# Blockwise attention before a mixture of experts: q and k loaded as runs of six tokens into 128 partitions, two heads' queries interleaved

## The chip, the cores and the metric

One core of one Trainium2 chip runs the whole program in one launch. The time is device microseconds of that launch, from the first to the last instruction of the core and what lies around it. Lower is better. Every figure is the median of several runs, or comes from one execution that the hardware profiler recorded.

## The reference

Three things are computed, one after the other: attention in chunks with some context and memory, a mixture of eight experts of which each token takes one, and a dense feed-forward layer.

```python
B, H, S, D = 4, 8, 768, 64            # chunk 32, context 16 to the left and 8 to the right, 8 memory keys
for c in range(S // 32):
    k_full = concatenate([mem_k, k[:, :, 32*c-16 : 32*c+40]])
    v_full = concatenate([mem_v, v[:, :, 32*c-16 : 32*c+40]])
    scores = matmul(q[:, :, 32*c : 32*c+32], k_full.T) / sqrt(D)
    a = exp(scores - max(scores)); a = a / (sum(a) + 1e-9)
    out[:, :, 32*c : 32*c+32] = matmul(a, v_full)
x = out.transpose(0, 2, 1, 3).reshape(B * S, H * D)        # 3072 x 512
e = argmax(x @ w_gate + modality_bias[modality_id])
x = gate_w * (maximum(x @ w1[e], 0) @ w2[e])               # 8 experts, 512 -> 1024 -> 512
out = elu(x @ w_in) @ w_out                                # 512 -> 2048 -> 512
```

All tensors are float32.

## The kernel before

`program` (from line 1140) holds an `Attention`, a `Routing`, a `Moe` and a `Moe2` object. The order of all instructions is written out by hand: inside `tc.manual_schedule` each engine runs its instructions in the order in which the Python code issues them, and semaphores keep the dependences. DMAs issued with `nc.sync` stand in SP's queue in that same order.

**Items and units.** Attention works on 8 items, an item being one batch and four heads (`self.items`), and on 24 units, a unit being one third of an item's 24 chunks, 8 chunks (`self.units`). "Item 3" is the fourth. `Attention.run` (line 426) goes through the units. In each it issues scores (`sc`), the transposition and the product with v of earlier units (`tr`, `pv`), the softmax (`sm`, `exp`), and some steps of the next item's q and k, taken from the list `pend` by the table `pops`: all eight steps of item ix + 1 run during item ix.

**Loads.** `load_qk(ix, j)` (line 82) loads k (j = 0) or q (j = 1) of an item: 768 tokens of four heads. Each partition takes a run of RUN = 8 tokens of each head, so 768 / 8 = 96 partitions are filled, and a piece of memory that lies in one stretch is 8 tokens x 64 x 4 bytes = 2,048 bytes. The arena tile `ld`, 128 x 6,144 floats, holds three such buffers, used in turn. `start` loads k and q of item 0, v of item 0 and k of item 1. In `run`, at the first unit of item ix, the v of item ix + 1 and the k of item ix + 2 are loaded (k first where ix is 0). The q of item ix + 1 is loaded by `tsteps(ix)`, behind the four k steps, since its buffer is the one that k of item ix leaves. `load_v` (line 93) brings v in pieces of 256 bytes, in 10 DMAs an item, of which the two long ones write 32 partitions each; `copy_v` on POOL then copies the overlapping part of the windows.

**Steps.** `transposed` (line 218) turns a loaded head with TensorE, two tokens (128 floats) at a time: RUN / 2 = 4 transposes of 96 partitions into one bank of PSUM. `k_step` copies half of the bank to kT on ACT and half on DVE. `q_step` copies both halves to qT on ACT. `k_next` makes the second half of each chunk's key window (POOL, and ACT for the memory keys).

**The block diagonal of queries.** Two heads x = 0, 1 share a matmul: the upper 64 partitions of qT hold head 0, the lower ones head 1, and the columns of the other head are zero (`zeros`, line 124, once per buffer). qT is `[128, 2, NC, 2, CH]`: for each chunk 32 columns of head 0, then 32 of head 1. `sc` (line 253) uses these 64 columns as the weights of one matmul, so scores come out with the 32 queries of head 0 above the 32 of head 1. After the softmax `tr` transposes them into `pt`, and `pv` (line 296) takes each head's 32 adjacent columns of `pt` as the weights of its product with v.

**After attention.** The buffers of `ld` become three buffers of 2,048 floats for expert weights (`wr.give("raw", ...)`, line 766), in the order 1, 2, 0. `Moe.load_w` fills them from SP's queue, the first behind the last load of attention.

Of the kernel before, what the change touches and what calls it, by code (L numbers as in the profile page):

```python
# [7 lines left out]
FP32 = dt.float32  # L8
# [12 lines left out]
CH, NC, NM, WIN = 32, 24, 8, 64  # L21
LEFT, RIGHT = 16, 8
TOK = LEFT + CH + RIGHT
RUN = 8
E = 8
ROW = 513
SLOT, SMALL = 384, 256
# [9 lines left out]
class Banks:  # L37


    def __init__(self, *T):  # L40
        self.T, self.n = T, 0
# [11 lines left out]
class Attention:  # L53
# [28 lines left out]
    def load_qk(self, ix, j):  # L82

        b, Q = self.items[ix]
        t = self.arena["ld"].rearrange("p (s h x) -> p s h x", s=3, h=4)[0:self.S // RUN, (2 * ix + j) % 3]
        self.nc.sync.dma_start(out=t, in_=(self.k, self.q)[j][b, 4 * Q:4 * Q + 4].rearrange("h (p r) d -> p h (r d)", r=RUN))
        self.loads[ix, j] = t

# [43 lines left out]
    def start(self):  # L132
        nc, const, S, D, B, NT = self.nc, self.const, self.S, self.D, self.B, self.NT
        t = lambda shape, name, d=FP32: const.tile(shape, d, name=name)
        self.vw, self.qT, self.kT = [None] * 3, [None] * 2, [None] * 2
        for s in range(3):
            self.vw[s] = (const, self.last)[s].tile([128, 2, NC, 130], FP32, name=f"vw{s}") if s < 2 else self.arena["vw"].rearrange("p (a c e) -> p a c e", a=2, e=130)
        for s in range(2):
            p = (const, self.last)[s]
            self.qT[s] = p.tile([128, 2, NC, 2, CH], FP32, name=f"qT{s}")  # L140
            self.kT[s] = p.tile([128, 2, 2, LEFT + S + RIGHT], FP32, name=f"kT{s}")
        self.x = self.rk.tile([128, 6, 512], FP32, name="x")
        mk = self.x[:, 4, 0:128].rearrange("p (x d) -> p x d", d=64)
        self.memT = t([128, 4 * B, NM], "memT")
        zero = t([128, 1], "zero")
        for j in range(2):
            self.load_qk(0, j)
        for x in range(2):
            nc.scalar.dma_start(out=mk[:, x], in_=bass.AP(
                tensor=self.mem_k.tensor, offset=self.mem_k.offset + x * NM * D, ap=[[2 * NM * D, 4 * B], [D, NM], [1, D]]))  # L150
        ident = self.ident = self.K["ident"]
        identity(nc, const, ident)
        for s in range(3):
            self.v_edges(s)
        self.load_v(0)
        self.load_qk(1, 0)
        nc.vector.memset(zero, 0.0)
        self.zeros(0)
        self.v_blocks(0, 1, nc.gpsimd)
        nc.scalar.copy(out=self.vw[0][self.half[1], :, :, 0:65], in_=zero[self.half[1]].unsqueeze(2).unsqueeze(3).to_broadcast([64, 2, NC, 65]))  # L160
        nc.vector.memset(self.vw[0][self.half[0], :, :, 64:65], 1.0)
        self.zeros(1)
        self.wgp = self.rk.tile([128, 4, 32], FP32, name="wgp")
        nc.gpsimd.memset(self.wgp, 0.0)
        for hh in range(2):
            self.v_blocks(1, hh, nc.gpsimd)
        pm = self.ps_t.tile([128, 128], FP32, name="ps_qk")
        nc.tensor.transpose(pm, mk.rearrange("p x d -> p (x d)"), ident)
        nc.vector.tensor_copy(out=self.memT.rearrange("p n m -> p (n m)"), in_=pm)
        for st in self.tsteps(0):  # L170
            st()
        self.copy_v(0)
        nc.gpsimd.dma_start(out=self.wgp[:, :, 0:8], in_=self.wg.rearrange("(c p) e -> p c e", p=128))
        self.mi = self.x[0:NT, 5, 0:256].bitcast(I32).rearrange("t (p two) -> t p two", two=2)
        nc.gpsimd.dma_start(out=self.mi, in_=self.mid.bitcast(I32).rearrange("(t p two) -> t p two", p=128, two=2))
        self.mb = const.tile([128, 2, E], FP32, name="mb")
        nc.gpsimd.dma_start(out=self.mb.rearrange("p m e -> p (m e)"), in_=self.mbias.rearrange("m e -> (m e)").unsqueeze(0).to_broadcast([128, 2 * E]))
# [54 lines left out]

    def q_step(self, ix, x, y):
        ps = self.transposed(ix, 1, x, y)
        o = self.qT[ix % 2][self.half[x], y, :, x].rearrange("p c (i s r) -> p c i s r", r=2, s=RUN // 2)
        for r in range(2):
            self.nc.scalar.copy(out=o[:, :, :, :, r], in_=ps[self.half[r]].rearrange("p s (c i) -> p c i s", i=CH // RUN))

    def k_next(self, ix):

# [7 lines left out]
    def tsteps(self, ix):  # L248
        xy = [(x, y) for y in range(2) for x in range(2)]
        steps = [lambda a=a: self.k_step(ix, *a) for a in xy]  # L250
        return steps + [lambda: (self.k_next(ix), ix + 1 < len(self.items) and self.load_qk(ix + 1, 1), self.q_step(ix, *xy[0]))] + [lambda a=a: self.q_step(ix, *a) for a in xy[1:]]


    def sc(self, u, gg):
        ix, G = self.units[u]
        s = ix % 2
        if gg == 0:
            self.scs[u] = self.ps_s.tile([128, 4, 2, WIN], FP32, name="ps_sc")
        ps = self.scs[u]
        for y in range(2):  # L260
            for i in range(4):
                c = 8 * G + 4 * gg + i
                j = 64 * (i % 2)
                self.nc.tensor.matmul(out=ps[j:j + 64, 2 * gg + i // 2, y], lhsT=self.qT[s][:, y, c].rearrange("p x q -> p (x q)"), rhs=self.kT[s][:, y, :, CH * c:CH * c + CH],
                                      start=True, stop=True, tile_position=(0, j))

    def sm(self, u):
# [28 lines left out]
    def pv(self, u):  # L296
        nc = self.nc
        ix, G = self.units[u]
        b, Q = self.items[ix]
        pt = self.ptt.pop(u)  # L300
        po = self.ps_v
        for gg in range(2):
            for hp in range(2):
                for j in range(4):
                    nc.tensor.matmul(out=po[32 * j:32 * j + 32, gg, 130 * hp:130 * hp + 130], lhsT=pt[:, 2 * gg + j // 2, 64 * (j % 2) + 32 * hp:64 * (j % 2) + 32 * hp + 32],
                                     rhs=self.vw[ix % 3][:, hp, 8 * G + 4 * gg + j, :], start=True, stop=True, tile_position=(0, 32 * j))
        x = self.x[:, 2 * G:2 * G + 2]
        pw = po[:, :, 0:260].rearrange("p g (h e) -> p g h e", e=65)
        den = self.wk.tile([128, 2, 4], FP32, name="den")
        nc.vector.tensor_scalar(out=den, in0=pw[:, :, :, 64], scalar1=1e-9, scalar2=None, op0=ALU.add)  # L310
        nc.vector.reciprocal(out=den, in_=den)
        for gg in range(2):
            nc.vector.tensor_tensor(out=x[:, gg, 256 * Q:256 * Q + 256].rearrange("p (b a d) -> p a b d", d=64, a=2), in0=pw[:, gg, :, 0:64].rearrange("p (a b) d -> p a b d", a=2),
                                    in1=den[:, gg].rearrange("p (a b) -> p a b", a=2).unsqueeze(3).to_broadcast([128, 2, 2, 64]), op=ALU.mult)
# [111 lines left out]
    def run(self, more):  # L426
# [30 lines left out]
        for u in range(N):  # L457
            ix, G = self.units[u]
# [3 lines left out]
                for _ in range(min(pops[i], len(pend))):  # L462
                    pend.pop(0)()
            if G == 0:
                loads = [(self.load_v, ix + 1), (self.load_qk, ix + 2, 0)]
                for f, i, *a in loads[::-1] if ix == 0 else loads:
                    if i < NI:
                        f(i, *a)
            if G == 0 and ix + 1 < NI:
# [283 lines left out]
class Moe:  # L753


    def __init__(self, ctx, tc, banks, turn, arena, xs, rt, w1, w2, x2T, idd, ident):
        self.nc, self.tc, self.ctx = tc.nc, tc, ctx
        self.__dict__.update(xs=xs, rt=rt, w1=w1, w2=w2, x2T=x2T, idd=idd, ident=ident)
        self.wr, self.gp, self.wp, self.xp, self.hp, self.op = self.rings = [Ring(b) for b in (3, 2, 4, 2, 3, 1)]
        self.ps_x, self.ps_h = self.turns = turn, Banks(*banks[3:5])  # L760
        self.acc = [t[:, 0:SLOT] for t in (banks[2], banks[5], banks[6][:, 0], banks[6][:, 1])]
        self.W, self.X, self.R, self.G, self.Hd, self.raw = {}, {}, {}, {}, {}, {}
        self.N = {}


        self.wr.give("raw", *[arena["ld"][:, 2048 * i:2048 * i + 2048] for i in (1, 2, 0)])
        self.gp.give("G", *[arena["vw"][:, 3 * ROW * i:3 * ROW * i + 3 * ROW].rearrange("p (a c) -> p a c", c=ROW) for i in range(2)])
        self.op.give("x2o", arena["vw"][:, 6 * ROW:6 * ROW + KC * SLOT].rearrange("p (d n) -> p d n", n=SLOT))
        for n in ("xh", "xl", "whi1", "wlo1"):
            (self.xp if n[0] == "x" else self.wp).give(n, arena[n])  # L770
# [522 lines left out]
```

## Time and profile before

| | us |
|---|---|
| median of 3 runs | 1042.43 |
| fastest and slowest of them | 1040.51, 1044.9 |
| the profiled execution, whole | 1038.87 |
| its span, first to last instruction | 1037.1 |
| PE busy in the span | 982.1 (95%) |
| DVE, ACT, POOL busy | 571.0, 431.3, 212.7 |
| attention's first to last load of k or q issued (line 86) | 0.8 to 121.2 |
| attention's first to last scores matmul (line 264) | 17.0 to 165.5 |

The page of a profile cuts the span into 40 slices of some 26 us and gives each engine's busy share in tenths. Attention takes about the first seven. A timeline lists instructions of one engine in order of time; the bracket behind a row tells how long the engine stood idle before it and which instruction or transfer ended that. The granted clock is the share of TensorE's full speed that the chip gave. TensorE's weight load (PEld) and matmul (PE) are separate records, and a float32 matmul that is no transpose appears as two of each.

### The profile page before, as it was taken

To read this page: it belongs to the slowest core of one execution; us is meant where nothing else is said; L and a number is where in the kernel's file an instruction comes from. 1 tells how busy PE (TensorE), PEld (TensorE's weight loads), DVE (VectorE), ACT (ScalarE), POOL (GpSimd) and SP (SyncE) were. 2 spreads that over 40 slices of the span, in tenths; PEclk is the share of its full clock that TensorE was granted. 3 is DMA by queue.
4 is the path that set the end of the run, shared out by engine and by line. 5 is a ranking of instruction groups with operands and counts; after the bars stand their busy time and mean duration, and the time that the engine had idled before them with its cause. 6 is when DMAs were issued, how large, how long until landed. Compare 5 with 4: busy or idle time off the path is not lost.

```text
span 1037.1 us, 16438 instructions
## 1 busy us (share of the span) xinstructions
PE 982.1 (95%) x6350; PEld 845.1 (81%) x6350; DVE 571.0 (55%) x1056; ACT 431.3 (42%) x797; POOL 212.7 (21%) x202
## 2 busy tenths in 40 slices
PE   5778979989999999999999999999999999999998
PEld 4656667879999999999778888888888888888886
DVE  5536677857998999755555333333333433343332
ACT  5656656355666566555444222222222222222221
POOL 7565451532432432310000000010010001001001
PEclk9889989999999999999999999999999999999999
DMA  9999982388978987775433100010110001001001
GB/s 176 138 203 162 215 216 70 85 273 295 340 274 289 354 303 272 237 228 182 147 101 112 41 31 21 21 41 1 41 41 1 0 1 41 1 1 41 1 1 41
DMA packets 95969, 130.59 MB, mean 126 GB/s; under 512 B 36586, under 2 KB 65340, under 8 KB 93832
## 3 DMA queue, kind: packets, MB, share of 16 engines
q1 hardware_dynamic: 85176, 97.56, 35.0%
q0 software_dynamic: 8816, 29.71, 8.5%
q10 hardware_dynamic: 1888, 2.16, 0.6%
q8 instruction: 53, 0.87, 0.4%
q14 instruction: 36, 0.29, 0.1%
HBM read 101.59 MB, written 27.81 MB: 125 GB/s over the span
## 4 chain that ended last, share of the span: by engine, by line
issue 32%; PE 17%; POOL 2%; POOLq 0%; ACT 0%; DVE 0%; ACTq 0%
PE b L1060 9%; PE b L1078 8%; POOL out_dram L1087 2%; POOLq L1287 0%; DVE g L1066 0%; ACT g L1064 0%; ACT o L1084 0%; DVE g L1065 0%; POOLq L1087 0%; PE b L1096 0%; ACT gh L1069 0%; ACTq L1084 0%; ACTq L1064 0%
## 5 line engine op out<-in xcount | busy, mean ns | idle before, releaser
L1065 DVE TENSOR_SCALAR g<-g 128x512 f32<-128x512 f32 x96 | 41.0, 427 | 247.7 <-ACT g L1064 247.5
L1064 ACT ACTIVATE g<-b 128x512 f32<-128x512 f32 x96 | 57.3, 597 | 260.8 <-PE b L1060 260.8
L1078 PE MATMUL b<-woh,gl 128*128 128x512 f32 x384 | 152.0, 396 | 0.0
L1078 PE MATMUL b<-woh,gh 128*128 128x512 f32 x384 | 152.0, 396 | 0.0
L1078 PE MATMUL b<-wol,gh 128*128 128x512 f32 x384 | 151.8, 395 | 0.0
L1087 POOL DMA_INDIRECT out_dram<-o,idc x24 | 23.4, 976 | 549.3 <-ACT o L1084 337.0
L1069 ACT CAST gh<-g 128x512 fp32r<-128x512 f32 x96 | 59.6, 621 | 118.0 <-DVE g L1066 118.0
L1060 PE MATMUL b<-c_xh,wih 128*128 128x512 f32 x384 | 104.4, 393 | 2.0 <-PEq L1243 2.0
L1060 PE MATMUL b<-c_xh,wil 128*128 128x512 f32 x384 | 103.9, 392 | 0.0
L1060 PE MATMUL b<-c_xl,wih 128*128 128x512 f32 x384 | 103.9, 392 | 0.0
L1070 DVE TENSOR_TENSOR gl<-g,gh 128x512 fp32r<-128x512 f32 x96 | 66.5, 693 | 65.9 <-ACT gh L1069 37.1
L858 PE MATMUL b<-hh,whi 128*128 128x384 f32 (+1 forms) x288 | 95.0, 330 | 0.8 <-ACT xT L331 0.8
L858 PE MATMUL b<-hl,whi 128*128 128x384 f32 (+1 forms) x288 | 94.7, 329 | 0.0
L858 PE MATMUL b<-hh,wlo 128*128 128x384 f32 (+1 forms) x288 | 94.6, 328 | 0.0
L807 DVE TENSOR_TENSOR wlo<-arena_ld,whi 128x512 fp32r<-128x512 f32 x128 | 85.4, 707 | 11.5 <-ACT whi L806 11.0
L1060 PEld LDWEIGHTS b<-c_xh,wih 128*128 128x128 f32 x384 | 72.0, 188 | 19.0 <-issue 2.2
L1078 PEld LDWEIGHTS b<-wol,gh 128*128 128x128 f32 x384 | 72.2, 188 | 17.5
L1078 PEld LDWEIGHTS b<-woh,gl 128*128 128x128 f32 x384 | 72.2, 188 | 17.4
L1078 PEld LDWEIGHTS b<-woh,gh 128*128 128x128 f32 x384 | 72.1, 188 | 17.1
L1060 PEld LDWEIGHTS b<-c_xl,wih 128*128 128x128 f32 x384 | 72.1, 188 | 16.3
L1060 PEld LDWEIGHTS b<-c_xh,wil 128*128 128x128 f32 x384 | 72.1, 188 | 16.3
L847 ACT ACTIVATE hh<-b 128x384 fp32r<-128x384 f32 (+1 forms) x72 | 34.5, 479 | 93.6 <-PE b L843 92.3
(248 smaller groups left out, 1687.9 us busy)
## 6 DMA issues: line engine op xcount, KB each, us to landing
arena_ld<-in_moe_w_dram SPq DMA_DIRECT2D x74, 512.0 KB
d<-in_moe_w_in_dram SPq DMA_DIRECT2D x8, 1024.0 KB
d<-in_moe_w_out_dram SPq DMA_DIRECT2D x8, 1024.0 KB
arena_ld<-in_k_dram SPq DMA_DIRECT2D x8, 768.0 KB
arena_ld<-in_q_dram SPq DMA_DIRECT2D x8, 768.0 KB
xs<-x POOLq DMA_DIRECT2D x12, 512.0 KB, 7.4
x2T<-arena_vw SPq DMA_DIRECT2D x32, 192.0 KB
vw<-in_v_dram SPq DMA_DIRECT2D x12, 376.0 KB
```

The lines of the kernel that those rows point to most:

```text
L807: self.nc.vector.tensor_tensor(out=lo[:, c], in0=r, in1=hi[:, c].bitcast(FP32), op=ALU.subtract)
L847: nc.scalar.activation(out=hh, in_=ps, func=ACTF.Relu)
L858: self.nc.tensor.matmul(out=self.acc[d][:, 0:self.N.get(s, SLOT)], lhsT=a[:, c:c + 128], rhs=b, start=f == 0 and i == 0, stop=f == NF - 1 ...
L1060: nc.tensor.matmul(out=ps, lhsT=a[:, kc, 128 * r:128 * r + 128], rhs=x[:, kc], start=n == 0, stop=n == 11)
L1064: nc.scalar.activation(out=g, in_=ps, func=ACTF.Exp)
L1065: nc.vector.tensor_scalar(out=g, in0=g, scalar1=1.0, scalar2=-1.0, op0=ALU.min, op1=ALU.add)
L1069: nc.scalar.copy(out=gh, in_=g)
L1070: nc.vector.tensor_tensor(out=gl, in0=g, in1=gh.bitcast(FP32), op=ALU.subtract)
L1078: self.nc.tensor.matmul(out=self.acc[t], lhsT=a[:, c], rhs=w[:, r], start=f == 0 and i == 0, stop=f == self.NF2 - 1 and i == 2)
L1087: ins = nc.gpsimd.indirect_dma_start(out=self.out, out_offset=bass.IndirectOffsetOnAxis(ap=self.idc[:, 4 * b + t:4 * b + t + 1], axis=0), ...
```

## The change

RUN becomes 6: 768 / 6 = 128 partitions are filled and a piece is 6 x 64 x 4 = 1,536 bytes. The tile `ld` is cut into four buffers of 1,536 floats instead of three of 2,048: one for k and one for q of even items, and the same of odd items. So q no longer waits for the buffer of the k one item before it, and `load_qk` leaves `tsteps`: `run` loads k and q of item ix + 2 together, behind v of item ix + 1, or ahead of it where ix is 0. A step has 3 transposes of 128 partitions. qT becomes `[128, 2, S, 2]`: for each token the column of head 0, then that of head 1. So the copies into it write every fourth float (every second before), the zeros every second float, and the weights of `pv` are every second column of `pt`. The buffers for expert weights are handed over in the order 0, 1, 2.

```diff
-RUN = 8
+RUN = 6
...
     def load_qk(self, ix, j):
         b, Q = self.items[ix]
-        t = self.arena["ld"].rearrange("p (s h x) -> p s h x", s=3, h=4)[0:self.S // RUN, (2 * ix + j) % 3]
+        t = self.arena["ld"].rearrange("p (s j h x) -> p s j h x", s=2, j=2, h=4)[:, ix % 2, j]
...
-            self.qT[s] = p.tile([128, 2, NC, 2, CH], FP32, name=f"qT{s}")
+            self.qT[s] = p.tile([128, 2, S, 2], FP32, name=f"qT{s}")
...
         self.load_v(0)
-        self.load_qk(1, 0)
+        for j in range(2):
+            self.load_qk(1, j)
...
     def q_step(self, ix, x, y):
         ps = self.transposed(ix, 1, x, y)
-        o = self.qT[ix % 2][self.half[x], y, :, x].rearrange("p c (i s r) -> p c i s r", r=2, s=RUN // 2)
+        o = self.qT[ix % 2][self.half[x], y, :, x].rearrange("p (i s r) -> p i s r", r=2, s=RUN // 2)
         for r in range(2):
-            self.nc.scalar.copy(out=o[:, :, :, :, r], in_=ps[self.half[r]].rearrange("p s (c i) -> p c i s", i=CH // RUN))
+            self.nc.scalar.copy(out=o[:, :, :, r], in_=ps[self.half[r]].rearrange("p s i -> p i s"))
...
-        return steps + [lambda: (self.k_next(ix), ix + 1 < len(self.items) and self.load_qk(ix + 1, 1), self.q_step(ix, *xy[0]))] + [lambda a=a: self.q_step(ix, *a) for a in xy[1:]]
+        return steps + [lambda: (self.k_next(ix), self.q_step(ix, *xy[0]))] + [lambda a=a: self.q_step(ix, *a) for a in xy[1:]]
...
-                ... lhsT=self.qT[s][:, y, c].rearrange("p x q -> p (x q)"), ...
+                ... lhsT=self.qT[s][:, y, CH * c:CH * c + CH].rearrange("p q x -> p (q x)"), ...
...
-                    ... lhsT=pt[:, 2 * gg + j // 2, 64 * (j % 2) + 32 * hp:64 * (j % 2) + 32 * hp + 32], ...
+                    ... lhsT=pt[:, 2 * gg + j // 2, 64 * (j % 2) + hp:64 * (j % 2) + 64:2], ...
...
             if G == 0:
-                loads = [(self.load_v, ix + 1), (self.load_qk, ix + 2, 0)]
-                for f, i, *a in loads[::-1] if ix == 0 else loads:
+                qk = [(self.load_qk, ix + 2, j) for j in range(2)]
+                v = [(self.load_v, ix + 1)]
+                for f, i, *a in v + qk if ix else qk + v:
...
-        self.wr.give("raw", *[arena["ld"][:, 2048 * i:2048 * i + 2048] for i in (1, 2, 0)])
+        self.wr.give("raw", *[arena["ld"][:, 2048 * i:2048 * i + 2048] for i in range(3)])
```

SP's queue around the v of item 1, which is `vw1`. The rows are those of k1, q1, k2, then v of item 1 and q2; in brackets stands the semaphore that the DMA waits for, PE's where its buffer must first have been transposed:

```order
-L86 DMA arena_ld_89<-in_k_dram 96x4x512 [waits DMAHW6_49]
-L86 DMA arena_ld_89<-in_q_dram 96x4x512 [waits DMAHW7_49,PE_49]
-L86 DMA arena_ld_89<-in_k_dram 96x4x512 [waits DMAHW0_49,PE_49]
-L101 DMA vw1_111<-in_v_dram 32x47x64 [waits DMAHW1_49]
...
+L86 DMA arena_ld_89<-in_k_dram 128x4x384 [waits DMAHW6_49]
+L86 DMA arena_ld_89<-in_q_dram 128x4x384 [waits DMAHW7_49]
+L86 DMA arena_ld_89<-in_k_dram 128x4x384 [waits DMAHW0_49,PE_49]
+L86 DMA arena_ld_89<-in_q_dram 128x4x384 [waits DMAHW1_49,PE_49]
+L101 DMA vw1_111<-in_v_dram 32x47x64 [waits DMAHW2_49]
...
-L86 DMA arena_ld_89<-in_q_dram 96x4x512 [waits DMAHW3_49,PE_49]
```

q2 moved from behind all of v of item 1 to ahead of it, and q1 lost its wait for PE. From item 3 on the order of the loads is the same as before.

PE's queue in unit 2, while the steps of item 1 are made; `b0` to `b2` are the banks of PSUM that the steps use. Before:

```order
L291 MATMUL b5_84<-ident_68,p_268 128x128 x4
L223 MATMUL b0_79<-ident_68,arena_ld_89 128x96 x4
L223 MATMUL b1_80<-ident_68,arena_ld_89 128x96 x4
L264 MATMUL b3_82<-kT0_113,qT0_112 64x64 x8
L223 MATMUL b2_81<-ident_68,arena_ld_89 128x96 x4
```

And with the change, where lines stand one lower:

```order
L292 MATMUL b5_84<-ident_68,p_261 128x128 x4
L224 MATMUL b0_79<-ident_68,arena_ld_89 128x128 x3
L224 MATMUL b1_80<-ident_68,arena_ld_89 128x128 x3
L265 MATMUL b3_82<-kT0_113,qT0_112 64x64 x8
L224 MATMUL b2_81<-ident_68,arena_ld_89 128x128 x3
```

No step moved on PE; each has three transposes of 128 columns where it had four of 96.

## Rows read from the trace of the kernel before

**Rows 1.** The page, busy tenths in 40 slices of the span.

```profile
PE   5778979989999999999999999999999999999998
...
DMA  9999982388978987775433100010110001001001
```

**Rows 2.** Waits of PE, 0 to 182 us: us in total, times, longest.

```profile
PE b L223 <- DMA arena_ld<-in_q_dram: 2.9, 1, 2.9
```

**Rows 3.** Timeline of SP's queue: start us, us, instruction.

```profile
16.84 0.31 SPq L86 DMA_DIRECT2D arena_ld<-in_k_dram  x1
17.64 0.31 SPq L101 DMA_DIRECT2D vw<-in_v_dram  x1
...
37.26 0.32 SPq L86 DMA_DIRECT2D arena_ld<-in_q_dram  x1
...
47.58 0.41 SPq L86 DMA_DIRECT2D arena_ld<-in_k_dram  x1
```

**Rows 4.** Line 86 by itself: duration ns min/median/max, first and last start us.

```profile
L86 SPq DMA_DIRECT2D arena_ld<-in_k_dram x8: 312/318/467, 0.8 to 119.0; - x8
```

**Rows 5.** Transfers, 19 to 28 us, in 40 slices.

```profile
GB/s 118 182 273 264 273 219 228 191 237 273 237 255 191 228 218 237 255 200 237 273 246 209 200 237 273 237 246 219 219 237 282 228 182 233 292 226 246 133 129 131
```

**Rows 6.** Transfers, 168 to 174 us, in 40 slices, and what was issued.

```profile
GB/s 0 0 0 0 0 0 0 0 61 205 198 232 280 375 396 369 369 382 355 259 109 137 164 150 164 273 396 396 423 314 369 328 232 109 0 0 0 0 0 0
...
arena_ld<-in_moe_w_dram SPq DMA_DIRECT2D x2, 512.0 KB
```

**Rows 7.** Timeline of PE, 57 to 70 us, [idle before <-what ended it].

```profile
57.00 0.90 PE L223 MATMUL b<-ident,arena_ld 96*128 96x96 f32 x4 [5.10 <-DMA arena_ld<-in_k_dram]
...
59.93 1.96 PE L305 MATMUL b<-vw,pt 128*32 128x130 f32 x32
...
64.86 0.69 PE L264 MATMUL b<-kT,qT 128*64 128x64 f32 x16
65.47 0.55 PE L223 MATMUL b<-ident,arena_ld 96*128 96x96 f32 x4
65.95 0.69 PE L264 MATMUL b<-kT,qT 128*64 128x64 f32 x16
66.57 0.66 PE L291 MATMUL b<-ident,p 128*128 128x128 f32 x4
67.06 0.38 PE L352 MATMUL b<-ident,ls 128*128 128x128 f32 x2
67.37 1.09 PE L305 MATMUL b<-vw,pt 128*32 128x130 f32 x32
68.40 1.09 PE L330 MATMUL b<-ident,x 128*128 128x128 f32 x8
```

**Rows 8.** Busy time by stretch; last three columns: granted clock, DMA share, GB/s.

```profile
core 0: us, PE busy (x) PEld busy (x) DVE busy (x) ACT busy (x) POOL busy (x), PEclk, DMA share, GB/s
...
57.00:64.00 7.00, 7.00 (x71) 5.82 (x72) 3.15 (x8) 2.02 (x4) 6.43 (x14) 0.55 1.25 134
64.00:94.00 30.00, 26.26 (x449) 19.88 (x447) 19.09 (x60) 21.66 (x45) 14.21 (x15) 1.00 1.03 199
```

**Rows 9.** Timeline of POOL, 30 to 40 us.

```profile
35.55 2.70 POOL L110 COPY vw<-vw 24x3008 f32<-24x3008 f32 x1 [6.94 <-DMA vw<-in_v_dram]
```

**Rows 10.** Single lines, 0 to 185 us: ns min/median/max, first and last start, shape.

```profile
L264 PEld LDWEIGHTS b<-kT,qT x768: 132/138/232, 17.0 to 165.5; 128*64 128x64 f32 x192
...
L305 PEld LDWEIGHTS b<-vw,pt x576: 106/110/178, 26.9 to 177.0; 128*32 128x32 f32 x192
...
L237 ACT COPY qT<-b x64: 474/496/523, 14.9 to 156.3; 64x384 f32<-64x384 f32 x64
...
L829 ACT CAST arena_xh<-b x4: 478/482/499, 160.1 to 161.9; 128x384 fp32r<-128x384 f32 x4
...
L130 DVE MEMSET qT<- x4: 1338/1338/1338, 3.6 to 8.8; 64x1536 f32 x4
...
L161 DVE MEMSET vw<- x1: 98/98/98, 6.7 to 6.7; 64x48 f32 x1
```

More of the change, by code (lines that the diff above doesn't have):

```diff
@@ L263, in sc @@
                 j = 64 * (i % 2)
-                self.nc.tensor.matmul(out=ps[j:j + 64, 2 * gg + i // 2, y], lhsT=self.qT[s][:, y, c].rearrange("p x q -> p (x q)"), rhs=self.kT[s][:, y, :, CH * c:CH * c + CH],
+                self.nc.tensor.matmul(out=ps[j:j + 64, 2 * gg + i // 2, y], lhsT=self.qT[s][:, y, CH * c:CH * c + CH].rearrange("p q x -> p (q x)"), rhs=self.kT[s][:, y, :, CH * c:CH * c + CH],
                                       start=True, stop=True, tile_position=(0, j))
@@ L304, in pv @@
                 for j in range(4):
-                    nc.tensor.matmul(out=po[32 * j:32 * j + 32, gg, 130 * hp:130 * hp + 130], lhsT=pt[:, 2 * gg + j // 2, 64 * (j % 2) + 32 * hp:64 * (j % 2) + 32 * hp + 32],
+                    nc.tensor.matmul(out=po[32 * j:32 * j + 32, gg, 130 * hp:130 * hp + 130], lhsT=pt[:, 2 * gg + j // 2, 64 * (j % 2) + hp:64 * (j % 2) + 64:2],
                                      rhs=self.vw[ix % 3][:, hp, 8 * G + 4 * gg + j, :], start=True, stop=True, tile_position=(0, 32 * j))
```

## The prediction

> **What bounds the kernel now.** I read the page's slices first. From the tenth of the 40 slices (26 us each) PE reads 9 to the end; in the first six it reads 5 to 9 while DMA reads 9, 9, 9, 9, 9, 8 [rows 1]. So there are two stages: attention, fed by transfers, and a long one that PE fills without gaps. The change touches the first only; the second follows in PE's order and moves by as much as the first ends earlier. I found no transfer in it that is due at a fixed time: its weight loads queue behind attention's own.
>
> Within attention I asked what ends PE's waits. Two name the loads that the change alters: 2.9 us for a q load [rows 2] and 5.1 us for a k load, the k of item 3 ("k3") [rows 7]. The loads are late because the queue is full: k2 and q2 of the same item are issued 20 us apart, with the v of item 1 between them, and k3 at 47.58 is the seventh load by then (k0, q0, k1, q1, k2, q2, k3) [rows 3]. From k3 to k7 k loads follow each other at (119.0 - 47.58) / 4 = 17.9 us [rows 3, 4], with no more PE waits on them. [...]
>
> **Part 1, the shape of a load.** A load keeps its 786,432 bytes: 384 pieces of 2,048 bytes into 96 partitions become 512 of 1,536 into 128. While k1, q1 and k2 fill the queue the engines move 182 to 292 GB/s, mean 236 over the plateau [rows 5]: 3.3 us a load. No load of 1,536 bytes into 128 partitions is in the trace; the nearest are the two weight loads at 168 to 174 us, 512 KB each into all 128 partitions in pieces of 1,024 and 2,048 bytes, which hold 355 to 396 and 314 to 423 GB/s [rows 6]. At 380 a load takes 2.1 us. Since the piece lengths on both sides of 1,536 run at that rate, I take 2.1, a saving of 1.2 us a load. Ends: nothing (236 stays), and 423 GB/s, 1.86 us, a saving of 1.5. Seven loads up to k3: 8.4 us (0 to 10.5).
>
> The rows alone do not say why 96 partitions are slow. [...]
>
> **Part 2, the order of the loads.** q2 now goes ahead of the v of item 1. PE's 2.9 us wait for q2 should go. What is late next is that v: POOL waited 6.9 us for it and copied it from 35.55 on [rows 9]. Before, five loads ran ahead of it (5 x 3.3 = 16.5 us); now six do (6 x 2.1 = 12.6), so it comes 3.9 us earlier, not later. If loads stay at 3.3 us it comes 3.3 us later, and PE's k3 wait of 5.1 us covers that. The count of issues on SP is the same.
>
> **What the two are worth.** k3 was there at 57.00 and PE had been ready for it 5.10 us before, at 51.9 [rows 7]. Without the q2 wait and with some of the shorter transposes (next part; 1.3 us of the first three items') PE is ready at about 51.9 - 2.9 - 1.3 = 47.7; k3 is there at 57.0 - 8.4 = 48.6. So a wait of about a microsecond is left and the gain is set by the load: 8.4 us. After a wait that short the clock may stay up: PV of one unit took 1.96 us after the wait and 1.09 later [rows 7]; in the 7 us at 0.55 some 3 us of work were lost [rows 8]. I take 1.5, ends 0 and 3.
>
> **Part 3, PE's transposes.** 64 steps issue 3 transposes instead of 4, 256 becoming 192. Four of 96 columns hold PE from 65.47 to 65.95, 0.48 us; four of 128 columns of p hold it from 66.57 to 67.06, 0.49 us [rows 7]. The length hardly counts, the number does: three cost 0.37, a saving of 0.11 a step. The 24 steps of items 0 to 2 lie in front of the k3 wait and are counted above. The other 40 give 4.4 us if PE paces those items; it also waits on other engines there, so I take 3 (0 to 4.4).
>
> **Part 4, strided weights for PV.** The weights of a PV matmul are now every second column, 8 bytes apart; no weight load in the trace is strided. A PV pair of load and matmul takes (68.40 - 67.37) / 32 = 32 ns; a scores pair, whose load reads 64 adjacent columns, the same span as 32 strided ones, takes (65.47 - 64.86) / 16 = 38 ns [rows 7]. There are 768 such pairs, some 590 of them after k3. Ends: nothing, and 6 ns each, 3.5 us. I take 1 us lost, since the load lies beside the matmul before it.
>
> **What I cost at nothing.** ACT's 64 copies into qT write 16 bytes apart instead of 8, 384 elements each as before; at 8 bytes they take 496 ns, and a copy of 384 adjacent elements 482 [rows 10]. No row has 16. ACT was busy 21.7 of 30 us [rows 8], which covers a little more; the far end is a rival below. The four memsets of qT (1,338 ns for 1,536 elements) write 8 bytes apart; a memset of 48 elements 520 bytes apart took 98 ns [rows 10], so spacing does not show, and they lie in the time in which the first loads arrive. Were they twice as long, 5 us of the start would go, into the k3 wait. Copies of k: the same element counts, ACT and DVE.
>
> **Sum.** 8.4 + 1.5 + 3 - 1 = 11.9 us. The profiled execution took 1038.87 us (span 1037.1 and 1.8 around it), so 1027.0 beside it; the median of the three runs is 1042.43, 3.6 above it, and against that the forecast is **1030.5**.
>
> **Rivals.**
> B, the load is no faster: 236 GB/s has another cause (the source rows, say). Against it stands the plateau at 380 [rows 6]. k3 then arrives at 57.0 as before, the q2 wait only becomes a longer k3 wait, and the shorter transposes run into k loads 17.9 us apart. Gain 0 to 2: 1041.4.
> C, ACT becomes the bound: a qT copy costs twice, 0.5 us more. Eight an item are 4 us of each 17.9, or 6.7 in 30: ACT 28.4 of 30 us, nearly full. In items 0 to 2 that is 12 us at most, PE ready for k3 between 47.7 and 59.7; with half of it exposed item 3 starts at 53.7, a gain of 3.3, clock 1.5, no gain from transposes, less 1: 1038.6. For it speaks that the trace has no write so spaced. [...]
> D, slower: the strided weight load becomes PE's bound. 32 columns more made a load 28 ns longer (138 against 110) [rows 10]. If each strided column costs two and nothing of it is hidden, 768 x 28 = 21.5 us are lost: 1042.4 - 12.9 + 21.5 = 1051. It decides from 12.9 / 768 = 17 ns a load; against it stands the scores pair at 38 ns for all of its 64 columns.
>
> **Chances.** Measurement tells about 0.5% (5 us) from no change. Forecast 0.74, its own range 1024 to 1035 (the upper ends of parts 1 to 3 together give 17; the price of part 4 and slower loads the other end); B 0.10; C 0.10; D 0.06. Range 1023 to 1040: it leaves out B and D. Faster takes the forecast, but for a small tail of weak savings, and nearly half of C: 0.77; same the rest of these and B, 0.17; slower D, 0.06.
>
> **What would show it.** In the profile after: k1, q1, k2, q2 on a plateau near 380 GB/s (right) or 236 (B); k3's transposes from 48 to 50 us with a wait of 0 to 2 us (right) or at 57 (B); the granted clock in the 7 us behind them above 0.55; three transposes in 0.37 us; qT copies near 500 ns (right) or 800 and more (C); PV in 1.0 to 1.2 us (right) or 1.9 (D). Wrong altogether if the time to k3 shrinks and the end does not: then something behind it was due at its own time.

## The result: slower, and the profile after

| | before, us | after, us |
|---|---|---|
| median of the comparison | 1042.11 | 1046.88 |
| fastest and slowest | 1040.28, 1044.9 | 1045.97, 1050.83 |
| span of the profiled execution | 1037.1 | 1044.4 |
| attention's last group of scores matmuls starts | 164.60 | 171.25 |

The ratio is 1.0055, with an interval of 1.0035 to 1.0075. The forecast was 1030.5, in a range of 1023 to 1040; the change is 4.8 us slower than before, and 16.4 us slower than forecast. A profile is of one execution, and executions of one kernel differ by some microseconds; the profiles of two experiments below, the interleaving without the loads and the copies shared with DVE, are of their longest ones, 1056.4 and 1051.09 us.

The loads did what was forecast. First the page's slices of the changed kernel, then its transfers from 19 to 28 us, which answer to [rows 1] and [rows 5]:

```profile
PE   4777888989999999999899999999999999999998
...
DMA  9997672268878987866432110010100001001001
```

```profile
GB/s 396 362 376 389 355 369 376 382 375 375 369 362 375 382 375 376 341 396 369 375 382 362 375 362 382 286 283 154 233 156 135 156 129 131 104 123 83 133 116 110
```

The plateau stands at 341 to 396 GB/s where it was at a mean of 236, and the six slices of DMA that read 9, 9, 9, 9, 9, 8 now read 9, 9, 9, 7, 6, 7. The load of k3 is issued earlier, at 41.53 instead of 47.58 us, and v of item 1 also comes earlier, as a row of SP's and one of POOL's timeline show:

```profile
41.53 0.74 SPq L86 DMA_DIRECT2D arena_ld<-in_k_dram  x1
```

```profile
31.15 2.70 POOL L110 COPY vw<-vw 24x3008 f32<-24x3008 f32 x1 [0.52 <-DMA vw<-in_v_dram]
```

But PE is no better off: in its slices 2 to 6 it reads 7, 7, 7, 8, 8 where it read 7, 7, 8, 9, 7. Its waits up to 182 us (us in total, times, longest) say why:

```profile
PE b L265 <- ACT qT L238: 15.3, 9, 3.2
...
PE b L224 <- ACT qT L238: 5.2, 6, 1.2
```

No wait for a load of k or q is left (they were 2.9 and 5.1 us, [rows 2, 7]). In their place PE waits 20.5 us for ACT's copies into qT: the scores matmuls for their queries, and the transposes for a bank of PSUM that such a copy still reads. Before, these two waits were 2.6 and 0.9 us:

```profile
PE b L264 <- ACT qT L237: 2.6, 4, 1.2
...
PE b L223 <- ACT qT L237: 0.9, 2, 0.5
```

The copies themselves, with the copies into kT on both engines beside them (duration in ns min/median/max, first and last start, shape; [rows 10] has the line of before):

```profile
L238 ACT COPY qT<-b x64: 822/847/902, 13.6 to 162.6; 64x384 f32<-64x384 f32 x64
```

```profile
L232 ACT COPY kT<-b x32: 472/502/517, 9.0 to 149.7; 64x384 f32<-64x384 f32 x32
L232 DVE COPY kT<-b x32: 559/561/564, 10.5 to 150.2; 64x384 f32<-64x384 f32 x32
```

A copy into qT takes 847 ns where it took 496, for the same 384 elements in each of 64 partitions. The copies into kT read a bank of the same form in the same order, but write 8 bytes apart, and did not change (502 and 561 ns before too).

Is ACT full? The view by stretch (columns as in [rows 8]) says no:

```profile
26.00:52.00 26.00, 20.66 (x324) 15.87 (x324) 19.66 (x40) 19.41 (x31) 13.46 (x8) 0.87 1.14 152
52.00:78.00 26.00, 20.46 (x297) 14.96 (x296) 10.87 (x28) 20.10 (x33) 15.93 (x20) 0.93 1.07 194
```

ACT, the fourth number behind the length, is busy 19.4 and 20.1 of 26 us. What hurts is where the copies stand. The timelines of ACT and of PE at the end of item 1, with the idle time before a row in brackets:

```profile
47.50 1.74 ACT L238 COPY qT<-b 64x384 f32<-64x384 f32 x2 [0.45 <-PE b L224]
49.04 0.63 ACT L286 ACTIVATE p<-p 128x512 f32<-128x512 f32 x1
49.70 3.47 ACT L238 COPY qT<-b 64x384 f32<-64x384 f32 x4
53.20 0.59 ACT L294 COPY pt<-b 128x512 f32<-128x512 f32 x1
53.81 1.66 ACT L238 COPY qT<-b 64x384 f32<-64x384 f32 x2
```

```profile
51.82 0.45 PE L265 MATMUL b<-kT,qT 128*64 128x64 f32 x8
55.52 0.45 PE L265 MATMUL b<-kT,qT 128*64 128x64 f32 x8 [3.25 <-ACT qT L238]
55.90 0.55 PE L224 MATMUL b<-ident,arena_ld 128*128 128x128 f32 x3
...
58.45 1.75 PE L306 MATMUL b<-vw,pt 128*32 128x130 f32 x32
```

All eight copies of item 2's queries follow each other in the last part of item 1 (47.50 to 55.47), with two other ACT instructions between them. They take 6.9 us; before, the same eight took 4.0, of which this row shows four that take 3.47 in the change:

```profile
46.31 2.03 ACT L237 COPY qT<-b 64x384 f32<-64x384 f32 x4
```

The next thing in PE's queue is the second half of unit 6's first scores, which needs the last of the eight. ACT may idle before and after; in these 8 us it sets the pace. The eight copies take 2.8 us longer than before, and PE's wait here is 3.25 us where it was 0.68, so nearly all of it is a delay of PE. k3 had arrived by then: its transposes (55.90) follow without a wait. And behind the 3.25 us in which PE stood, PV runs slowly, 1.75 us for a unit that takes 1.09 elsewhere; the 7 us from 55.5 have a granted clock of 0.76. So k3's transposes are a mere 1.1 us earlier than before (55.90 against 57.00), where 8.4 were forecast, and the wait, 2.69 us already at the end of item 0 (37.3 us), recurs at the boundaries of later items: 0.71, 1.10, 0.71, 2.67 and 0.72 us at 77.5, 96.0, 118.0, 139.1 and 163.5 us.

### The profile page after: what moved, and what is told of

It reads as the page before. It is cut to its first block, busy times and chain, and to the rows that moved or that the text cites. A ratio compares the mean times of both kernels' runs of the same rounds, so it can differ in the third digit from the quotient of the medians.

```text
span 1044.4 us, 16302 instructions
## 1 busy us (share of the span) xinstructions
PE 986.2 (94%) x6286; PEld 844.7 (81%) x6286; DVE 575.9 (55%) x1056; ACT 453.7 (43%) x797; POOL 212.9 (20%) x202
## 4 chain that ended last, share of the span: by engine, by line
issue 32%; PE 18%; POOL 2%; POOLq 0%; ACT 0%; DVE 0%; ACTq 0%
PE b L1062 9%; PE b L1080 8%; POOL out_dram L1089 2%; POOLq L1289 0%; DVE g L1068 0%; ACT g L1066 0%; ACT o L1086 0%; DVE g L1067 0%; POOLq L1089 0%; PE b L1098 0%; ACT gh L1071 0%; ACTq L1086 0%; ACTq L1066 0%
```

## The experiments

My theory when the runs began: the loads are worth about what the forecast says, and the 16-byte spacing of the writes into qT takes it back, through ACT's copies. The rivals: the slow copies come from the order in which they read the bank, not from their writes; the strided weights of PV or the order of the loads costs something; or the loads are worth little, because something behind them is due at its own time.

### The loads without the interleaving

The change, with the old layout of qT. Its copies read PSUM exactly as in the change; they write 8 bytes apart, and PV's weights are adjacent columns again.

```diff
-            self.qT[s] = p.tile([128, 2, S, 2], FP32, name=f"qT{s}")
+            self.qT[s] = p.tile([128, 2, NC, 2, CH], FP32, name=f"qT{s}")
...
-        o = self.qT[ix % 2][self.half[x], y, :, x].rearrange("p (i s r) -> p i s r", r=2, s=RUN // 2)
+        o = self.qT[ix % 2][self.half[x], y, :, x].rearrange("p c (m r) -> p c m r", r=2)
...
-                ... lhsT=self.qT[s][:, y, CH * c:CH * c + CH].rearrange("p q x -> p (q x)"), ...
+                ... lhsT=self.qT[s][:, y, c].rearrange("p x q -> p (x q)"), ...
...
-                    ... lhsT=pt[:, 2 * gg + j // 2, 64 * (j % 2) + hp:64 * (j % 2) + 64:2], ...
+                    ... lhsT=pt[:, 2 * gg + j // 2, 64 * (j % 2) + 32 * hp:64 * (j % 2) + 32 * hp + 32], ...
```

> The change with the query tile of before (32 columns of head 0, then 32 of head 1, ACT writes 8 bytes apart); the loads of six tokens, the four buffers and the order of the change stay. Theory A (the 16-byte spacing of ACT's writes into qT made the copies 847 ns and took the gain of the loads): copies back at 490 to 530 ns, PE's waits for qT back from 15 us to about 3, time 1026 to 1035 us. Rival B (the copies are slow because a bank is now read as 128 x 3 instead of 96 x 4): copies stay near 847 ns, time 1044 to 1049. Rival C (the order of the loads is what costs): copies near 500 ns, and the time still 1042 or more.

Measured: 1032.9 against 1042.57 of the kernel before, ratio 0.9907 (0.9891 to 0.9922). It is faster than both kernels, by 9.7 and by 14.0 us. (The change was timed beside another series of the kernel before, with a median of 1042.11; each taken against its own series, the second number is 14.4.) Its copies into qT, its waits of PE, and PE's timeline around k3:

```profile
L238 ACT COPY qT<-b x64: 472/498/536, 13.6 to 148.7; 64x384 f32<-64x384 f32 x64
```

```profile
PE b L265 <- ACT qT L238: 5.4, 6, 1.5
...
PE b L224 <- ACT qT L238: 1.1, 2, 0.7
```

```profile
47.14 0.45 PE L265 MATMUL b<-kT,qT 128*64 128x64 f32 x8 [0.85 <-ACT qT L238]
48.45 0.55 PE L224 MATMUL b<-ident,arena_ld 128*128 128x128 f32 x3 [0.85 <-DMA arena_ld<-in_k_dram]
48.92 0.69 PE L265 MATMUL b<-kT,qT 128*64 128x64 f32 x16
...
50.12 1.09 PE L306 MATMUL b<-vw,pt 128*32 128x130 f32 x32
```

The copies are back at 498 ns with the reading order of the change, so that order is not what costs. k3's transposes run at 48.45 us after a wait of 0.85; the forecast had 48.6 and "about a microsecond". The clock stays up: PV takes 1.09 us, and the 7 us from 48.45 have a granted clock of 1.00. PE waits 6.5 us for qT against the change's 20.5, so 14.0 us less (of 15.3 us in the scores 5.4 are left, where about 3 were expected); the spans differ by 14.7 (1029.7 and 1044.4). That the two differences nearly agree is not exact evidence: the run with writes 48 bytes apart, below, waits the same 20.5 us and has a span of 1040.5.

### The interleaving without the loads

Before, with the tile, the copies, the zeros and the weights of the change; loads of eight tokens in the old order.

```diff
-            self.qT[s] = p.tile([128, 2, NC, 2, CH], FP32, name=f"qT{s}")
+            self.qT[s] = p.tile([128, 2, S, 2], FP32, name=f"qT{s}")
...
-        o = self.qT[ix % 2][self.half[x], y, :, x].rearrange("p c (i s r) -> p c i s r", r=2, s=RUN // 2)
+        o = self.qT[ix % 2][self.half[x], y, :, x].rearrange("p (i s r) -> p i s r", r=2, s=RUN // 2)
...
```

> The kernel before with the interleaved query tile alone: runs of eight tokens into 96 partitions, three buffers and the old order stay. Theory A: qT copies 820 to 880 ns, 64 times 0.35 us more on ACT, part of it hidden under the waits for k and q that are still there: 1047 to 1056 us. Rival B: copies stay at 496 ns and the time at 1040 to 1044.

Measured: 1052.13, ratio 1.0085 (1.0066 to 1.0104), so 9.6 us slower. The copies take 846 ns, and PE's waits are these:

```profile
PE b L264 <- ACT qT L237: 17.5, 9, 3.2
...
PE b L223 <- ACT qT L237: 5.1, 6, 1.2
...
PE b L223 <- DMA arena_ld<-in_k_dram: 0.7, 1, 0.7
```

PE's wait for k3 has shrunk from 5.1 us to 0.7, and the one for q2 is gone: PE comes to the loads later. k3's transposes start at 57.20 us, where they started at 57.00 before:

```profile
57.20 0.90 PE L223 MATMUL b<-ident,arena_ld 96*128 96x96 f32 x4 [0.70 <-DMA arena_ld<-in_k_dram]
```

So up to there the late loads hide the slower copies, and that is why the same copies cost 9.6 us here and 14.0 on top of the faster loads.

### Which part of the loading it is

Before, with runs of six tokens into 128 partitions, in three buffers and the old order, and the old layout of qT.

```diff
-RUN = 8
+RUN = 6
...
-        t = self.arena["ld"].rearrange("p (s h x) -> p s h x", s=3, h=4)[0:self.S // RUN, (2 * ix + j) % 3]
+        t = self.arena["ld"].rearrange("p (s y) -> p s y", s=3)[:, (2 * ix + j) % 3, 0:1536].rearrange("p (h x) -> p h x", h=4)
...
```

> The kernel before with runs of six tokens into 128 partitions alone: three buffers, the order of the loads and the query tile are those of before. Theory A with the loads as the source of the gain: loads near 375 GB/s instead of 236, the 5.1 us wait for k of item 3 gone or under 2 us, 1028 to 1035 us, at most 3 us behind the run with the new order as well. If the order is what helps, most of the wait for q of item 2 (2.9 us) stays and the time is 1037 or more.

Measured: 1033.93, ratio 0.9917 (0.9899 to 0.9936). The shape alone brings 8.6 of the 9.7 us; what the fourth buffer and the order add (1.0 us) is within the two intervals. PE's wait for q2 is gone here too, so it does not take the new order to remove it. k3 comes at 50.89 us, 6.1 earlier than before, after a wait of 2.52 (at most 2 had been expected), and PV behind it runs at 1.96 us:

```profile
50.89 0.90 PE L223 MATMUL b<-ident,arena_ld 128*128 128x128 f32 x3 [2.52 <-DMA arena_ld<-in_k_dram]
```

The order and the fourth buffer are worth 2.4 us more at that place (48.45), and PV at 1.09. Most of this is lost again. PE's timeline in the first experiment, of three units whose PV starts at 67.37 [rows 7], 80.11 and 86.71 us before:

```profile
56.05 1.09 PE L306 MATMUL b<-vw,pt 128*32 128x130 f32 x32
...
70.76 1.09 PE L306 MATMUL b<-arena_vw,pt 128*32 128x130 f32 x32 [1.88 <-DVE x L314]
...
79.30 1.96 PE L306 MATMUL b<-arena_vw,pt 128*32 128x130 f32 x32
```

It leads the kernel before by 11.3, 9.4 and 7.4 us, and by 7.6 at attention's last scores (156.99 against 164.60). PE waits at 70.76 for DVE, whose instruction writes x anew and had itself stood 5.79 us, until 69.95, for a transfer of x to memory (`xs<-x`); a stretch of slower matmuls follows, with 16 of the scores in 1.12 us from 77.20 on where they take 0.69 from 72.59. With the shape alone the lead is 6.0 us at all these places, and the same DVE instruction starts at 69.92, after a wait of 0.42. That transfer ended at 69.9 in both runs: the earlier k3 reached it, and gained little behind it.

### The copies shared with DVE

The change, with half of the copies into qT on DVE, as for kT.

```diff
-            self.nc.scalar.copy(out=o[:, :, :, r], in_=ps[self.half[r]].rearrange("p s i -> p i s"))
+            cp = self.nc.vector.tensor_copy if r else self.nc.scalar.copy
+            cp(out=o[:, :, :, r], in_=ps[self.half[r]].rearrange("p s i -> p i s"))
```

> The change, with every second copy into qT on DVE instead of ACT. It asks whether the spacing costs on ACT alone. If so, DVE's copies take about 560 ns as its copies of k do, ACT loses 4 x 0.85 us an item, and the time comes to 1032 to 1040 us. If DVE pays as ACT does, its copies take 800 to 950 ns, and the time stays at 1040 to 1048.

Measured: 1046.53, ratio 1.0045 (1.0028 to 1.0061): no gain over the change. The copies, and PE's wait for them:

```profile
L239 ACT COPY qT<-b x32: 822/852/921, 13.6 to 165.4; 64x384 f32<-64x384 f32 x32
L239 DVE COPY qT<-b x32: 831/852/908, 14.5 to 166.3; 64x384 f32<-64x384 f32 x32
```

```profile
PE b L266 <- DVE qT L239: 20.8, 8, 11.3
```

DVE pays as well: 852 ns where the same copy into kT, 8 bytes apart, takes it 561. Two engines halve the work, and seven of these eight waits come to 9.5 us, where nine came to 15.3 in the change. But DVE has its own work in front of these copies: in the eighth, of 11.3 us, instructions of the routing stand between two of them. Whether that wait is as long in other executions is not shown.

### Does the cost grow with the distance?

Two runs give the spacing other values; theory A is still that a wider spacing of the writes made the copies slow. The change, whose copies now walk the tokens of one bank column by column, so that their writes are 48 bytes apart:

```diff
-            self.nc.scalar.copy(out=o[:, :, :, r], in_=ps[self.half[r]].rearrange("p s i -> p i s"))
+            self.nc.scalar.copy(out=o[:, :, :, r].rearrange("p i s -> p s i"), in_=ps[self.half[r]])
```

> The change, with each copy into qT running over the bank in its own order, so that neighbouring reads are adjacent and neighbouring writes stand 48 bytes apart instead of 16. [...] If the cost grows with the distance: over 1000 ns. If it was the reading across the bank that cost: under 600 ns.

And the kernel before, old layout of qT, whose copies write the same places in another order, 32 bytes apart:

```diff
-            self.nc.scalar.copy(out=o[:, :, :, :, r], in_=ps[self.half[r]].rearrange("p s (c i) -> p c i s", i=CH // RUN))
+            self.nc.scalar.copy(out=o[:, :, :, :, r].rearrange("p c i s -> p s c i"), in_=ps[self.half[r]].rearrange("p s (c i) -> p s c i", i=CH // RUN))
```

> The kernel before with its own query tile and loads; only the copies into qT run over the bank in its own order, so that neighbouring writes stand 32 bytes apart instead of 8. Theory A: copies 820 to 880 ns though no layout changed, and the time goes up as with the interleaved tile alone, 1047 to 1056 us. If the interleaved tile costs through something else (the weights of PV, the zeros): the time stays under 1045.

The copies of the first and of the second (duration in ns min/median/max):

```profile
L238 ACT COPY qT<-b x64: 812/830/865, 13.6 to 158.7; 64x384 f32<-64x384 f32 x64
```

```profile
L237 ACT COPY qT<-b x64: 790/808/841, 14.9 to 165.0; 64x384 f32<-64x384 f32 x64
```

On ACT a copy takes 496 ns with its writes 8 bytes apart, 847 at 16 bytes, 808 at 32 (a little under the 820 expected) and 830 at 48: the price appears somewhere between 8 and 16 bytes, and beyond that does not grow with the distance. 12 bytes were not tried, and why the writes cost more there is not shown. On DVE two spacings were tried, with 561 ns at 8 bytes and 852 at 16. The copies at 32 and 48 bytes also read the bank in its own order, and with the reading order of the change but 8 bytes between writes the first experiment had 498, so the reading is not what costs. The second run measured 1051.09, ratio 1.0083 (1.0053 to 1.0113): slower copies alone, with the old layout, the old loads and adjacent weights, cost 8.5 us, about as much as the whole interleaving did (9.6). That leaves little for the interleaved weights to cost. Of the first there is one time, 1042.44 us, too little to compare by; PE's waits are those of the change (15.3 and 5.2 us).

### What the rate of a load depends on

Is it the partitions, or the length of a piece? The kernel before, each load as two DMAs into the same 96 partitions, with pieces of 1,024 bytes:

```diff
-        self.nc.sync.dma_start(out=t, in_=(self.k, self.q)[j][b, 4 * Q:4 * Q + 4].rearrange("h (p r) d -> p h (r d)", r=RUN))
+        for a in range(2):
+            s = (self.k, self.q)[j][b, 4 * Q:4 * Q + 4].rearrange("h (p a r) d -> p h a (r d)", a=2, r=RUN // 2)
+            self.nc.sync.dma_start(out=t[:, :, 256 * a:256 * a + 256], in_=s[:, :, a])
```

> The kernel before with each load of k and q split into two, with pieces of 1,024 bytes instead of 2,048, still into 96 partitions. Theory: the number of partitions sets the rate, so the plateau of loads stays near 236 GB/s (220 to 250). Rival: the length of a piece sets it, and the plateau moves by 20% or more, up or down.

And the first experiment's kernel, each load as two DMAs of 64 partitions:

```diff
-        self.nc.sync.dma_start(out=t, in_=(self.k, self.q)[j][b, 4 * Q:4 * Q + 4].rearrange("h (p r) d -> p h (r d)", r=RUN))
+        s = (self.k, self.q)[j][b, 4 * Q:4 * Q + 4].rearrange("h (p r) d -> p h (r d)", r=RUN)
+        for a in self.half:
+            self.nc.sync.dma_start(out=t[a], in_=s[a])
```

> The faster kernel (loads of six tokens, four buffers, new order, old query tile) with each load split into two, one for partitions 0 to 63 and one for 64 to 127; the pieces stay at 1,536 bytes. Theory: a transfer is as fast as the partitions that it reaches at one time allow, so the plateau falls from 375 GB/s to about half, 180 to 230. Rival: any 16 engines' worth of rows run at 375: the plateau stays above 330.

The transfers of the first from 19 to 28 us, and of the second from 20 to 29:

```profile
GB/s 114 155 214 232 259 205 232 255 200 196 228 228 232 205 246 269 205 205 218 232 232 228 264 255 182 287 214 255 200 237 296 191 218 205 246 215 220 254 174 166
```

```profile
GB/s 184 198 205 198 205 184 218 205 225 225 212 212 191 191 205 191 273 225 205 205 198 198 205 212 232 239 212 205 218 178 205 205 218 259 218 198 203 184 221 155
```

With half the piece the rate stays where it was, at some 230. With 64 partitions in each DMA, though 128 are filled in the end, it falls to 208 in the mean. Both runs split a load into two DMAs of the same size, so it is not the split. Nor is it the number of pieces: a DMA of the second run has 256, and so has the load of 512 KB in pieces of 2,048 bytes that held 314 to 423 GB/s into 128 partitions [rows 6]. These rates go with the number of partitions that one DMA reaches, though not in proportion: 208, 236 and 375 for 64, 96 and 128. One time of each, 1043.73 and 1038.95 us, fits that and settles no more; in the second PE waits for k loads again, 6.0 us in three places.

## Why the prediction was wrong, step by step

**What bounds the kernel: right for the first items.** The two waits for loads were what held PE there; with the q2 wait gone and 0.85 us left of the k3 wait, and the old layout of qT, the end came 9.7 us earlier. That the rest "moves by as much as the first ends earlier" did not hold within attention: by the profiles a lead of 11.3 us shrank to 7.6, from a transfer of x on that ended at 69.9 us with either order and that the prediction did not have.

**Part 1, the shape: right in the rate, lucky in the place.** A load takes 2.1 us, from a plateau near 375 GB/s, and rival B falls with it. k3 was there at 48.45 us in the first experiment, 48.6 forecast. But the forecast put all 8.4 us down to seven shorter loads, and the shape alone moved k3 by 6.1; the other 2.4 came with the order and the fourth buffer, which it had not counted there. PE was ready for k3 at 47.6 us, 47.7 forecast, and this too is in part luck: the 1.3 us laid to shorter transposes came from the granted clock behind the vanished q2 wait, where PE's work from q2's transposes to the wait for k3 took 7.7 us at a clock of 0.78 before and 6.4 at 1.00 in the first experiment.

**Part 2, the order: right on v, and worth little at the end.** v of item 1 comes 4.4 us earlier in the change and 3.9 in the first experiment (3.9 forecast). The q2 wait is gone, but the shape alone removes it as well. Beside the shape, the order adds about 1 us, which is not clear of the noise.

**Clock: right at k3 without the interleaving.** After a wait of 0.85 us the granted clock was 1.00, and the lead grew from 8.6 us at k3's transposes to 11.3 at 56.05 us, so by some 2.8, where 1.5 were forecast; they are part of the lead that was lost again after 70 us. In the change the clock was 0.76 there: another wait, of 3.25 us, stood in the place of the one removed.

**Part 3, the transposes: wrong.** I put three at 0.37 us, four at 0.48. The changed kernel's timeline has a step of three from 44.22 us on:

```profile
44.22 0.55 PE L224 MATMUL b<-ident,arena_ld 128*128 128x128 f32 x3
44.69 0.69 PE L265 MATMUL b<-kT,qT 128*64 128x64 f32 x16
```

0.47 us for three, and before 0.48 for four [rows 7]. The 3 us of this term were nothing. I had taken the length of a transpose not to count, from four of 128 columns in 0.49 us; by the same rows neither does the number between three and four. I overlooked that a step turns the same 384 columns either way, 3 x 128 or 4 x 96. Eight of 96 (23.43 to 24.24 us before) and six of 128 (46.92 to 47.72 after) have 768 columns each and take 0.81 and 0.80 us; eight of 128 take 0.93 (68.40 [rows 7] to 69.33 before). So the length does count, and these times go with the columns rather than with the number of transposes. The four of 128 in 0.49 us do not fit that, and no run was made to separate the two. In the weight-load queue the three loads end after 0.31 us, and the next group starts 0.17 us later with nothing that the profile names; why the step does not end sooner was not tried.

**Part 4, strided weights: its 1 us was nothing.** A weight load at 8 bytes takes what it took, and PV 1.09 us a unit. Rival D falls.

```profile
L306 PEld LDWEIGHTS b<-vw,pt x576: 107/110/178, 28.9 to 183.7; 128*32 128x32 f32 x192
```

**"What I cost at nothing": the step that failed.** The memsets stayed at 1,338 ns. The copies into qT did not stay near 500 ns: they took 847. "No row has 16" was true, and I took the free end, from the copies at 8 bytes and at 4 (496 and 482 ns), which differ by 14 ns. Both spacings lie below the one asked about, and two such times say nothing of 16 bytes and more, where the runs had 808 to 852 ns.

**Rival C had the cause and the wrong price.** It put 0.5 us on a copy, and 0.351 was measured: 64 x 0.351 = 22.5 us of ACT's time. Of these 14.0 show at the end on top of the faster loads, 7.5 up to k3's transposes (55.90 against 48.45) and the rest behind them. C let half of three items' copies show, 6 of 12 us, and after item 3 let them cost no more than the gain from the transposes, because I judged ACT by its busy share, 21.7 of 30 us. But the eight copies of an item stand together, and the last is the one that the next unit's scores wait for. Had I seen that place, C's own price would have made it slower than before: an estimate by the measured share is 64 x 0.5 x 14.0 / 22.5 = 20 us lost, against the 11.9 gained.

**The sum, as it is.** Loads and order, minus 9.7 us; slower copies, plus 14.0; together 1042.57 - 9.7 + 14.0 = 1046.9, the median measured. That it comes out even is no evidence, since the 14.0 is the difference to the first experiment; the evidence is that each part was also run without the other: minus 8.6 for the shape alone, plus 9.6 for the interleaving alone, plus 8.5 for slow copies alone.

## What to carry to other kernels

Before a layout is changed, look at how far apart an engine's neighbouring writes come to lie: at 16 bytes instead of 8, a copy of float32 here took 1.7 times as long on ACT (847 ns against 496), at 32 and 48 bytes much as at 16 (808 and 830), and 1.5 times as long on DVE (852 against 561), where 8 and 16 bytes alone were tried. Ask of a slower instruction not how busy its engine is, but who waits for the last of the group that it stands in. And where a change has two parts, time each alone: here one gained 9.7 us, the other cost more, and the whole looked like a change that does harm. Last, a lead won early may not reach the end: here a third of it was lost from a transfer on that nothing had waited for before.

## What had not been expected of the hardware

A load into 128 partitions, in pieces of 1,536 bytes, ran at some 375 GB/s, one into 96 at some 230, with pieces of 1,024 as of 2,048 bytes, and two into 64 each at 208, in pieces of 1,536 bytes. Two halves do not add up to a whole, though both stand in the queue together. Why the rate goes with the partitions that one DMA reaches was not shown.

Three transposes of 128 columns took PE as long as four of 96, 0.47 and 0.48 us, and six as long as eight, 0.80 and 0.81.

That PE would load every second column as weights in 110 ns, as it did adjacent ones, while ACT's writes to every fourth float would take 847 ns instead of 496, was not foreseen either: the two strides, of 8 and of 16 bytes, were in the same change, and I feared for the wrong one. Weights 16 bytes apart were not tried.
